# An attention and MLP kernel: the rows' normalization factors gathered in one tile, turned by TensorE and stored in one transfer

## The chip, the cores and the metric

The kernel runs on one core of a Trainium2 chip. The metric is the device time of one execution in microseconds (us). The page of the profile and the trace come from one execution; the times of the runs stand beside it. Engines are named as in the profile: PE is TensorE (matrix products; PEld its weight loads), DVE is VectorE, ACT is ScalarE, POOL is GpSimd, and SP is SyncE, which here only issues transfers. A name with a q behind it (SPq, POOLq) is that engine's issuing of transfers.

## What is computed

For 2048 rows of 640 features, a normalized copy of the input goes into two branches, and both are added to the input. One branch is attention with 32 heads of 20 features, the other a second normalization and a two-layer network of width 1536 with GELU.

```python
def reference(A_x, A_wqkv, A_wo, B_x, B_w1, B_b1, B_w2, B_b2):
    x = A_x                                   # 1 x 2048 x 640
    xn = _layernorm(x, axis=-1)
    return x + _A_ref(xn, A_wqkv, A_wo) + _B_ref(xn, B_w1, B_b1, B_w2, B_b2)

    # _A_ref: softmax(q k^T / sqrt(20)) v per head, times wo
    # _B_ref: y = _layernorm(x); gelu(y w1 + b1) w2 + b2
```

The second normalization works on rows that are normalized already, so it is one factor per row. That factor is applied late, to the product with w1, and it is what this change is about.

## The kernel before

**Numbers in halves.** Most products are made of pairs of 16-bit floats (a high and a low half), three products each.

**The projection stage** takes about the first 224 us. The rows are handled in four chunks of 512 (c = 0 to 3). For each chunk a loop over tt = 0 to 4 makes five pairs of 128 output features of q and k (`qk`, 30 matrix products of 128x512, L337, into PSUM tiles `qkp`); behind it, a loop over j = 0 to 3 makes v for 128 rows at a time (`vproj`, 30 products of 128x320, L410, into tiles `vp`). Both use the PSUM pool `psS`, which has three buffers, so a product must wait until the tile three before it has been read. `qk_out` reads a finished `qkp`: ACT writes the high half (L352), DVE the low half (L353) into a tile `qkhl` of two buffers, and SP stores both halves to `qkscr` in HBM (L358). A new `qkhl` can be written only when the store of the one two before it has landed.

**The next chunk's rows** are made ready during a chunk. `norm_a`, `norm_b` and `norm_c` compute mean and variance of 4 x 128 rows, the first factor (tile `r`), the normalized rows, and the second factor (tile `r2`, 128 x 4: row 128 j + p of the chunk is at partition p, column j). `turn` splits normalized rows in halves (tile `row`, three buffers, L318 and L319) and turns them with a DMA transpose into `xnt` (L320), of which a copy goes to HBM (`xscr`, L323). Chunk 0 runs its own norm steps ahead of the loops and inside the first one; chunk 1's run in chunk 0, chunk 2's in chunk 1, chunk 3's in chunk 2.

**The weights** of the MLP are split into halves on ACT and DVE in small pieces between these steps (`some`, `weights`, `split`, L139 to L141); the output weights `wos` are fetched by POOL (L506) for their scale.

**The factors' way.** At the end of `norm_c`, POOL stores the chunk's 512 factors to the HBM tensor `rscr` (L286). In HBM they are to stand in the order of the rows, while in the tile neighbouring rows stand in neighbouring partitions, so the store consists of 512 elements of four bytes. `load_chunk` fetches 256 of them at a time (L1015), spread over all 128 partitions, as `r2f`. The first two loads are issued by SP at 220 us, ahead of the attention stage; L989 and L966 use them.

**The attention stage** (from about 224 us) makes scores (L748), exponentials on ACT (L750), low halves on DVE (L762) and the products with v (L779), 64 blocks of heads and rows; the MLP's two products (L1031 and L1061) are strewn between them by a plan that is fixed when the program is built. The output product (L1146) ends the kernel.

**Order.** The instructions of each engine run in the order in which the program is written (manual schedule); engines wait for each other through semaphores. SP's and POOL's transfers are issued in order too: a transfer whose inputs aren't ready holds those behind it.

Of the kernel before, what the change touches and what calls it, by code (L numbers as in the profile page):

```python
# [9 lines left out]
F32 = mybir.dt.float32  # L10
# [8 lines left out]
P = 128  # L19
S, D, H, DH, F = 2048, 640, 32, 20, 1536  # L20
KD = D // P
KF = F // P
NKB = S // P
# [16 lines left out]
MC = 256  # L40
# [4 lines left out]
def mha_mlp_kernel(tc, x, wqkv, wo, w1, b1, w2, b2, out):  # L45
    nc = tc.nc
# [3 lines left out]
    with (  # L50
# [8 lines left out]
    ):  # L59
        qkscr = dram.tile([2, 2 * D, S], F16, name="qkscr")  # L60
        xscr = dram.tile([P, KD, 2, S], F16, name="xscr")
        rscr = dram.tile([S], F32, name="rscr")
        oscr = dram.tile([2, D, S], F16, name="oscr")
        opart = dram.tile([2, D, S], F32, name="opart")
        lpart = dram.tile([2, 2, H, S // 2], F32, name="lpart")
# [13 lines left out]
        ident = keep.tile([P, P], F32, name="ident")  # L79
# [95 lines left out]
        with tc.tile_pool(name="pa", bufs=2) as pa, tc.tile_pool(name="pa1", bufs=1) as pa1, tc.manual_schedule():  # L175
# [59 lines left out]
                    nc.tensor.matmul(ps[:, :P], ones, ones, start=True, stop=True)  # L235

            rs = {}

            def newton(dst, v, pref, by=1.0):
                t = pa.tile([P, 4], F32, tag=pref + "t", name=pref + "t")  # L240
                nc.vector.tensor_mul(t, dst, dst)
                nc.vector.scalar_tensor_tensor(t, v, -0.5 * by, t, ALU.mult, ALU.mult)
                nc.vector.scalar_tensor_tensor(dst, t, 1.5 * by, dst, ALU.add, ALU.mult)

            def norm_a(c, between=None):

                xt = xts[c]
                st = pa.tile([P, 4, 2, 6], F32, tag="st", name="st")
                mv = pa.tile([P, 4, 2], F32, tag="mv", name="mv")
                ve = pa.tile([P, 4], F32, tag="ve", name="ve")  # L250
                r = pa.tile([P, 4], F32, tag="r", name="r")
                r2 = pa.tile([P, 4], F32, tag="r2", name="r2")
                for j in range(4):
                    for i in range(2):
                        nc.vector.bn_stats(st[:, j, i, :], xt[j][:, i * 320 : (i + 1) * 320])  # L255
                    nc.vector.bn_aggr(mv[:, j, :], st[:, j])
                nc.vector.tensor_scalar(ve, mv[:, :, 1], EPS, None, ALU.add)
                if c == 0:
                    between()
                    nc.scalar.activation(r, mv[:, :, 1], AF.Sqrt, bias=eps)  # L260
                    nc.vector.reciprocal(r, r)
                else:
                    nc.gpsimd.tensor_tensor(r, ve, nhalf, ALU.pow)
                rs[c] = mv, ve, r, r2
# [18 lines left out]
            def norm_c(c):  # L283
                mv, ve, r, r2 = rs.pop(c)
                newton(r2, ve, "b")
                nc.gpsimd.dma_start(rscr[c * 512 : (c + 1) * 512].rearrange("(j p) -> p j", p=P), r2)  # L286

            xnts = {}

# [56 lines left out]
            def qk_out(c, tt, ps):  # L346
                hl = stp.tile([P, 2, 2, 512], F16, tag="ks", name="qkhl")

                parts = ((0, 2),) if tt != 2 else ((0, 1), (1, 2))
                for i0, i1 in parts:  # L350
                    a = qks[:, (2 * tt + i0) // KD : (2 * tt + i0) // KD + 1]
                    nc.scalar.activation(hl[:, 0, i0:i1], ps[:, i0:i1], AF.Copy, scale=a)  # L352
                    nc.vector.scalar_tensor_tensor(hl[:, 1, i0:i1], ps[:, i0:i1], a, hl[:, 0, i0:i1],  # L353
                                                   ALU.mult, ALU.subtract)
                if c + tt > 0:
                    qk_sq(c, tt, hl)
                for s in range(2):
                    nc.sync.dma_start(  # L358
                        qkscr[s, 2 * tt * P : (2 * tt + 2) * P, c * 512 : (c + 1) * 512]
                        .rearrange("(i p) t -> p i t", p=P), hl[:, s])  # L360
                return hl

            def qk_sq(c, tt, hl):
                if tt % 2:
                    sq = stp.tile([P, S // 2], F16, tag="qs", name="sq").bitcast(BF16).rearrange("p (i t) -> p i t", i=2)
                else:
                    sq = pa.tile([P, 2, 512], BF16, tag="sq", name="sq", bufs=2)
                if c == 0:
                    nc.scalar.activation(sq, hl[:, 0], AF.Square)
                else:  # L370
                    nc.vector.tensor_mul(sq, hl[:, 0], hl[:, 0])
                pend.extend((c, 2 * tt + i, sq[:, i]) for i in range(2))
# [56 lines left out]
            def sums(tag, ws):  # L429
                accs[tag] = squares(ws, junk)  # L430
# [154 lines left out]
            for c in range(4):  # L585
                nxt = c + 1 if c < 3 else None
                for tt in range(5):
                    if c == 0 and tt == 1:
                        norm_b2(0)
                        norm_c(0)  # L590

                        nc.scalar.activation(junk[:, :1], ones[:, :1], AF.Exp)
                        ps = qk(0, 1, lambda: scale_of("k"))
                        hl = qk_out(0, 0, first)
                        split_qkv("q", c0=4 * P)
                        split_qkv("k")
                    else:
                        ps = qk(c, tt)
                    if tt == 3:
                        lengths(4)  # L600

                    if c == 0:
                        if tt == 0:
                            split_qkv("q", c0=2 * P, c1=4 * P)
                            sums("k", [stage["k"][:, 0:3], stage["k"][:, 3:]])
                            first = ps
                            continue
                        elif tt == 1:
                            qk_sq(0, 0, hl)
                        elif tt == 2:  # L610
                            sums("v", [stage["v"][:, 0:3], stage["v"][:, 3:]])
                            norm_a(1)
                        elif tt == 3:
                            scale_of("v")
                            split_qkv("v")
                    else:

                        step = tt - (c == 1)
                        if nxt and 0 <= step < 3:
                            (norm_a, norm_b, norm_c)[step](nxt)  # L620
                            some(1)
                        else:
                            some(2)
                    qk_out(c, tt, ps)

                    ask((0, 1, 2, 2, 1)[tt] if c == 0 else 0)
                    if nxt and c > 0 and tt >= 2:
                        for j in ((0,), (1, 2), (3,))[tt - 2]:
                            turn(nxt, j)
                    if c == 3 and tt == 2:  # L630
                        early = [load_features(mc) for mc in range(2)]
                if c == 1:
                    load_x(3)
                if c == 3:
                    stack = load_stack(0, 0)
                    for _ in range(6):
                        next(stack)
                for j in range(4):
                    ps = vproj(c, j)
                    if j == (0 if c == 3 else 1):  # L640
                        lengths(10)
                    if c + j > 0:

                        vproj_out(c, j, ps)
                    if c == 0:
                        if j < 2:
                            (norm_b, norm_c)[j](1)

                        pts = []
                        for k in ((), (0,), (2, 4), ())[j]:  # L650
                            transp(1, k, pts)
                        for t in pts:
                            transp_out(*t)
                    if j == 0 and c == 3:
                        shifts()
                        for _ in stack:
                            pass
                    some(1 if c == 3 else 2 if j < 3 or c == 0 else 0)
                    if c + j == 0:
                        vproj_out(c, j, ps)  # L660
                    if c == 0:
                        ask(2 if j == 0 else 1)
                if c == 0:
                    load_x(2)
# [3 lines left out]
        with ExitStack() as scope:  # L668
# [342 lines left out]
            def load_chunk(mc):  # L1011
                t0 = mc * MC
                xnt = early.pop(0) if early else load_features(mc)
                r2f = m1.tile([P, MC], F32, tag="r2f", name="r2f", bufs=2)
                nc.sync.dma_start(r2f, rscr[None, t0 : t0 + MC].to_broadcast([P, MC]))  # L1015
                xs[mc] = xnt, r2f
                unscaled.append(r2f)
                if mc > 1:
                    patient.append(scale_ahead(r2f))
# [323 lines left out]
```

The loop that calls them, cut:

```python
            for c in range(4):                                  # L585
                nxt = c + 1 if c < 3 else None
                for tt in range(5):
...
                        step = tt - (c == 1)
                        if nxt and 0 <= step < 3:
                            (norm_a, norm_b, norm_c)[step](nxt)
                            some(1)
                        else:
                            some(2)
                    qk_out(c, tt, ps)
```

## Time and profile before

| | us |
|---|---|
| runs (three) | 1332.33, 1337.95, 1342.94 |
| median | 1337.95 |
| profiled execution, span | 1337.9 |
| projection stage, 0 to 235 us: PE, DVE, ACT busy | 228.0, 146.2, 122.3 |
| attention, 235 to 1275 us: PE, DVE, ACT busy | 1039.6, 887.2, 1005.1 |
| end, 1275 to 1337.9 us: PE, DVE, ACT busy | 58.2, 21.6, 0.6 |
| mean granted clock of PE | 0.997 |

The profiled execution has no other time of its own than its span, which is within 0.05 us of the median of the runs. Busy time counts instructions at work, not waiting ones. "x12" behind a name is a count of instructions; "[3.67 <-DVE qkhl L353]" says that the engine was idle for 3.67 us before the instruction, and that an instruction of line 353 on DVE ended this.

### The profile page before, as it was taken

To read this page: it belongs to the slowest core of one execution; us is meant where nothing else is said; L and a number is where in the kernel's file an instruction comes from. 1 tells how busy PE (TensorE), PEld (TensorE's weight loads), DVE (VectorE), ACT (ScalarE), POOL (GpSimd) and SP (SyncE) were. 2 spreads that over 40 slices of the span, in tenths; PEclk is the share of its full clock that TensorE was granted. 3 is DMA by queue.
4 is the path that set the end of the run, shared out by engine and by line. 5 is a ranking of instruction groups with operands and counts; after the bars stand their busy time and mean duration, and the time that the engine had idled before them with its cause. 6 is when DMAs were issued, how large, how long until landed. Compare 5 with 4: busy or idle time off the path is not lost.

```text
span 1337.9 us, 29042 instructions
## 1 busy us (share of the span) xinstructions
PE 1325.8 (99%) x11635; PEld 586.7 (44%) x11635; DVE 1055.1 (79%) x1431; ACT 1128.0 (84%) x1306; POOL 37.5 (3%) x86
## 2 busy tenths in 40 slices
PE   9999899999999999999999999999999999999998
PEld 6645456444434343434343443344443434333366
DVE  7656754998788989878897879888879888997742
ACT  7844334999999999999999999999999999999900
POOL 3010000000000000000000000000000000000000
PEclk9999899999999999999999999999999999999999
DMA  9778723021203232212322132223032323334375
GB/s 279 254 196 176 136 79 104 15 59 39 66 28 103 61 83 81 63 48 59 111 63 81 33 93 66 75 69 94 19 80 71 93 66 87 118 95 118 105 218 188
DMA packets 100326, 129.54 MB, mean 97 GB/s; under 512 B 24292, under 2 KB 66664, under 8 KB 100188
## 3 DMA queue, kind: packets, MB, share of 16 engines
q1 hardware_dynamic: 96652, 120.25, 31.6%
q0 software_dynamic: 2912, 6.90, 2.8%
q8 instruction: 92, 1.51, 0.5%
q10 hardware_dynamic: 624, 0.51, 0.1%
q14 instruction: 46, 0.38, 0.1%
HBM read 82.14 MB, written 42.51 MB: 93 GB/s over the span
## 4 chain that ended last, share of the span: by engine, by line
PE 87%; DVE 6%; DMA 4%; ACT 1%; issue 1%; SPq 0%; ACTq 0%; DVEq 0%
PE o L779 30%; PE s L748 20%; PE py L1061 13%; PE pu L1031 11%; PE z L1146 5%; PE qkp L337 5%; PE vp L410 3%; DVE low L762 2%; DMA xt<-in_A_x_dram 1%; DMA xnt<-row 1%; DMA qkscr<-qkhl 1%; DVE st L255 1%; DVE qkhl L353 1%; ACT p L750 1%; DMA wos<-in_A_wo_dram 0%
## 5 line engine op out<-in xcount | busy, mean ns | idle before, releaser
L750 ACT ACTIVATE p<-s 128x1024 f32<-128x1024 f32 x1024 | 973.9, 1050 | 33.1 <-PE s L748 27.1
L762 DVE TENSOR_TENSOR low<-p 128x1024 f16<-128x1024 f32 x512 | 614.3, 1218 | 144.8 <-ACT p L750 144.0
L779 PE MATMUL o<-p,vfull 128*32 128x512 bf16 (+1 forms) x4096 | 429.0, 493 | 0.0
L748 PE MATMUL s<-qs,ks 61*128 61x512 f16 x2048 | 311.4, 381 | 0.2 <-ACT p L750 0.2
L748 PEld LDWEIGHTS <-ks 61*128 61x128 f16 x2048 | 61.2, 94 | 278.4 <-issue 276.1
L1061 PE MATMUL py<-w2t,hT 128*128 128x320 f16 x1152 | 178.5, 300 | 0.0
L1031 PE MATMUL pu<-xm,w1t 128*128 128x256 f16 x1440 | 178.2, 273 | 0.1
L1031 PEld LDWEIGHTS <-w1t 128*128 128x128 f16 x1440 | 131.0, 98 | 64.0 <-issue 50.2
L1061 PEld LDWEIGHTS <-hT 128*128 128x128 f16 x1152 | 102.3, 98 | 88.1 <-issue 53.9
L337 PE MATMUL qkp<-xnt,wv 128*128 128x512 f16 x600 | 131.1, 379 | 1.3 <-issue 1.3
L779 PEld LDWEIGHTS <-vfull 128*32 128x32 f16 x3072 | 59.9, 95 | 138.4 <-issue 106.9
L779 PE MATMUL o<-low,vfull 128*32 128x512 f16 x1024 | 101.3, 377 | 0.1
L337 PEld LDWEIGHTS <-wv 128*128 128x128 f16 x600 | 58.2, 98 | 71.0 <-issue 1.6
L779 PEld LDWEIGHTS o<-p,vfull 128*32 128x32 f32 x2048 | 61.7, 108 | 53.2
L410 PE MATMUL vp<-wv,xnt 128*128 128x320 f16 x480 | 69.5, 306 | 3.7 <-DVE qkhl L353 3.7
L1146 PE MATMUL z<-w1t,ot 128*128 128x320 f16 x480 | 67.4, 299 | 0.0
L352 ACT ACTIVATE qkhl<-qkp,qks 128x1024 f16<-128x1024 f32 (+1 forms) x24 | 23.1, 964 | 46.3 <-PE qkp L337 26.6
L410 PEld LDWEIGHTS <-xnt 128*128 128x128 f16 x480 | 47.9, 100 | 23.8 <-issue 3.7
L1146 PEld LDWEIGHTS <-ot 128*128 128x128 f16 x480 | 46.0, 98 | 22.9 <-issue 5.5
L353 DVE SCALAR_TENSOR_TENSOR qkhl<-qkp,qks,qkhl 128x1024 f16<-128x1024 f32 (+1 forms) x24 | 26.5, 1104 | 32.9 <-ACT qkhl L352 32.9
L1103 DVE SCALAR_TENSOR_TENSOR acc<-z,sc,acc 128x320 f32<-128x320 f32 x32 | 17.5, 549 | 37.3 <-PE z L1146 37.2
L800 ACT ACTIVATE ev<-o 128x512 f32<-128x512 f32 x64 | 39.5, 618 | 2.2 <-PE o L779 2.1
(195 smaller groups left out, 670.4 us busy)
## 6 DMA issues: line engine op xcount, KB each, us to landing
qkscr<-qkhl SPq DMA_DIRECT2D x40, 256.0 KB
opart<-ev SPq DMA_DIRECT2D x124, 80.0 KB
ks<-qkscr SPq DMA_DIRECT2D x120, 80.0 KB
qs<-qkscr SPq DMA_DIRECT2D x192, 40.0 KB
oa<-opart SPq DMA_DIRECT2D x32, 240.0 KB
xt<-in_A_x_dram SPq DMA_DIRECT2D x16, 320.0 KB
xscr<-xnt SPq DMA_DIRECT2D x4, 1280.0 KB
xm<-xscr SPq DMA_DIRECT2D x8, 640.0 KB
```

Of the source, the lines that this page charges most:

```text
L337: nc.tensor.matmul(ps[:, i, :], wv[:, k, q, a, mm * P : (mm + 1) * P], xnts[c][:, k, b, :], start=(k + n == 0), stop=(k == KD - 1 and n == 2))
L352: nc.scalar.activation(hl[:, 0, i0:i1], ps[:, i0:i1], AF.Copy, scale=a)
L353: nc.vector.scalar_tensor_tensor(hl[:, 1, i0:i1], ps[:, i0:i1], a, hl[:, 0, i0:i1], ALU.mult, ALU.subtract)
L410: nc.tensor.matmul(ps[:, hf, :320], xnts[c][:, k, a, j * P : (j + 1) * P], wv[:, k, 2, b, hf * 320 : (hf + 1) * 320], start=(n == 0), stop ...
L748: nc.tensor.matmul(ps[:, a, :], ks[64 * a : 64 * a + 61, kb * P : (kb + 1) * P], qs[64 * a : 64 * a + 61, cc * 512 : (cc + 1) * 512], star ...
L750: nc.scalar.activation(pt, ps, AF.Exp, scale=QS)
L762: nc.vector.tensor_sub(low, pt, upper(pt))
L779: nc.tensor.matmul(pv.o[32 * q : 32 * q + 32, :], src[:, v0 - PAD * (1 - q % 2) :][:, :32], t, start=q not in pv.begun, stop=last, skip_gr ...
L800: nc.scalar.activation(evs[g, hf][:, cc], pv.o, AF.Copy)
L1031: nc.tensor.matmul(ps[:, i], w1v[:, k, (f + i) // 4, a, fo_ : fo_ + P], xnt[:, k, b, :], start=(n == 0), stop=(n == 3 * KD - 1))
L1061: nc.tensor.matmul(ps[:, :320], hTs[mc][:, f, a, j * P : (j + 1) * P], w2v[:, f, b, hf * 320 : (hf + 1) * 320], start=(n == 0), stop=(n == ...
L1146: nc.tensor.matmul(ps[:, :320], ot[:, k, a, j * P : (j + 1) * P], wov[:, k, b, h * 320 : (h + 1) * 320], start=(n == 0), stop=(n == 3 * KD ...
```

## The change

`rscr` becomes a tensor of 16 x 128 (the same bytes in the same order). One tile `rall` of 128 x 16 takes the place of the four tiles `r2`: chunk c computes its factors in columns 4c to 4c+3. `norm_c` no longer stores. A new function, `factors_out`, is called once, in the last chunk behind the second group of q and k (c = 3, tt = 1): PE turns `rall` into a PSUM tile `pr` of 16 x 128, DVE copies it to `rrow`, and POOL stores that in 16 rows of 512 bytes. The eight loads of `r2f` read the same places as before.

```diff
-        rscr = dram.tile([S], F32, name="rscr")
+        rscr = dram.tile([NKB, P], F32, name="rscr")
...
             rs = {}
+            rall = pa1.tile([P, NKB], F32, name="rall")
...
-                r2 = pa.tile([P, 4], F32, tag="r2", name="r2")
+                r2 = rall[:, 4 * c : 4 * c + 4]
...
             def norm_c(c):
                 mv, ve, r, r2 = rs.pop(c)
                 newton(r2, ve, "b")
-                nc.gpsimd.dma_start(rscr[c * 512 : (c + 1) * 512].rearrange("(j p) -> p j", p=P), r2)
+
+            def factors_out():
+
+                pr = psM.tile([P, 512], F32, tag="m", name="pr")[:NKB, :P]
+                nc.tensor.transpose(pr, rall, ident)
+                rrow = sm.tile([NKB, P], F32, tag="rrow", name="rrow", bufs=1)
+                nc.vector.tensor_copy(rrow, pr)
+                nc.gpsimd.dma_start(rscr, rrow)
...
                     qk_out(c, tt, ps)
+                    if c == 3 and tt == 1:
+                        factors_out()
...
-                nc.sync.dma_start(r2f, rscr[None, t0 : t0 + MC].to_broadcast([P, MC]))
+                nc.sync.dma_start(r2f, rscr.rearrange("j p -> (j p)")[None, t0 : t0 + MC].to_broadcast([P, MC]))
```

Lines behind L285 carry numbers that are 8 higher in the changed kernel (L353 is L361 there), lines behind L624 numbers that are 10 higher.

## The prediction

> **What bounds the kernel now.** I read the head of the page first, then the waits of the first 235 us, the chain of waits there, stages of 4 us, and last the tile that the change touches.
>
> ```profile
> span 1337.9 us, 29042 instructions
> PE 1325.8 (99%) x11635; PEld 586.7 (44%) x11635; DVE 1055.1 (79%) x1431; ACT 1128.0 (84%) x1306; POOL 37.5 (3%) x86
> PEclk9999899999999999999999999999999999999999
> ```
>
> TensorE (PE) works 1325.8 of 1337.9 us, so only 12.1 us of the span is PE idle time. Whatever a change gains must come out of those 12.1 us or out of stretches with a lower clock, and the clock row dips once, in the fifth slice (134 to 167 us). That lies in the projection stage, where all four stores of the rows' factors lie too.
>
> ```profile
> ACT qkhl L352 <- DMA qkscr<-qkhl: 6.3, 1, 6.3
> PE vp L410 <- DVE qkhl L353: 3.7, 1, 3.7
> ACT row L318 <- DMA xnt<-row: 6.5, 1, 6.5
> ```
>
> These are waits of the first 235 us (total, times, longest). PE's largest wait in the stage, 3.7 us, is on VectorE (DVE), not on a transfer. The chain of waits leads further back; its columns are start, duration, what:
>
> ```profile
> 138.86 12.66 DMA qkscr<-qkhl
> ...
> 151.63 1.12 ACT qkhl L352
> ...
> 152.77 1.28 DVE qkhl L353
> ...
> 158.17 1.29 DVE qkhl L353
> ...
> 159.50 6.88 PE vp L410 x30
> ...
> 207.91 4.08 PE vp L410 x30
> ```
>
> A store of q and k halves (L358), issued at 138.86, needed 12.66 us. ScalarE (ACT) could not refill that buffer before 151.63; DVE then ran late through its queue, its next qkhl ended at 159.46, and the PSUM buffer that the second vp block needs came free only then. The block itself took 6.88 us, while 30 equal matmuls at 207.91 took 4.08.
>
> Why did a 256 KB store need 12.66 us? The stages show PE, weight load, DVE, ACT and POOL busy, then clock, DMA share, GB/s:
>
> ```profile
> 24.00:28.00 4.00, 4.00 (x22) 1.98 (x20) 2.56 (x11) 3.97 (x11) 0.81 (x1) 1.00 1.06 373
> 28.00:32.00 4.00, 4.00 (x21) 1.73 (x19) 4.00 (x9) 4.00 (x7) 0.00 (x0) 1.00 1.01 98
> ...
> 60.00:64.00 4.00, 4.00 (x34) 3.27 (x33) 0.27 (x2) 3.39 (x6) 0.00 (x0) 1.00 1.01 402
> 64.00:68.00 4.00, 4.00 (x30) 2.72 (x29) 2.14 (x6) 3.61 (x7) 0.00 (x0) 1.00 0.57 104
> ...
> 100.00:104.00 4.00, 4.00 (x31) 2.96 (x30) 3.13 (x15) 1.11 (x1) 0.00 (x0) 1.00 1.12 27
> ...
> 148.00:152.00 4.00, 4.00 (x21) 1.96 (x20) 0.00 (x0) 0.37 (x1) 0.00 (x0) 1.00 1.14 43
> ...
> 156.00:160.00 4.00, 0.50 (x3) 0.27 (x3) 3.93 (x8) 2.76 (x5) 0.00 (x0) 0.76 0.92 183
> 160.00:164.00 4.00, 4.00 (x17) 2.27 (x16) 3.79 (x13) 0.00 (x0) 0.00 (x0) 0.50 0.75 194
> 164.00:168.00 4.00, 4.00 (x47) 2.62 (x46) 2.12 (x6) 1.58 (x3) 0.00 (x0) 0.88 0.64 215
> ```
>
> ```profile
> L286 POOL DMA_DIRECT2D rscr<-r x4: 767/791/812, 24.6 to 140.2; - x4
> ...
> DMA to landing us min/median/max: 11.4/11.6/12.5
> ...
> 58.70 0.79 POOL L286 DMA_DIRECT2D rscr<-r  x1 [3.54 <-DVE r L243]
> ...
> 94.74 0.79 POOL L286 DMA_DIRECT2D rscr<-r  x1 [3.21 <-DVE lo L117]
> ```
>
> Four times the throughput falls to between 27 and 104 GB/s. Two of these times the share of busy DMA time is still above 1, so packets are under way and do not finish. The four stores of factors, 2 KB each as 512 elements of four bytes, were issued at 24.6, 58.70, 94.74 and 140.2, and each took 11.4 to 12.5 us: every drop lies inside one of them. Two of the four cost PE nothing that I can see: it is busy 4.00 of 4.00 at 28 to 32 and 64 to 68 us.
>
> **The change, part by part.** First the removed stores. The last one issues 1.3 us after the qkscr store that then needs 12.66 us. Gone with it is the 3.67 us of PE idle time, in the first row here (time, duration, work, idle time before it):
>
> ```profile
> 159.50 6.88 PE L410 MATMUL vp<-wv,xnt 128*128 128x320 f16 x30 [3.67 <-DVE qkhl L353]
> ...
> 118.66 3.61 PE L337 MATMUL qkp<-xnt,wv 128*128 128x512 f16 x16 [1.26 <-issue]
> ```
>
> and with it the clock loss behind the idle time: the block's 6.88 against 4.08 is 2.80 us. The stage table checks this: half clock for 4 us costs 2.0, 0.88 for 4 us another 0.5, and 0.50 us of work at a lower clock in the stage before about 0.25, together 2.7.
>
> The Trainium skill, "TensorE: Matmul & The Clock Gate", Part 1 (the HAM clock gate), says that PE falls to half its clock after an idle window of about 3.4 us. The trace agrees: 3.67 us idle was followed by a clock of 0.50, and 1.26 us idle by no dip.
>
> The third store (94.74) was in flight while ACT waited 6.5 us at 108 us for a DMA transpose to release its row buffer. The last transpose of the block of rows came late through that, and PE waited 1.26 us at 118.66 for it. I count that as gone too: ACT's 6.5 us of lateness is over five times the 1.26.
>
> What is late next where the stall was?
>
> ```profile
> 144.99 6.65 PE L337 MATMUL qkp<-xnt,wv 128*128 128x512 f16 x30
> ...
> 155.55 0.28 PE L114 MATMUL mxp<-acco,ones 128*128 128x5 f32 x2
> ```
>
> Without the wait ACT takes up qkhl about 6.3 us earlier, at 145.3 instead of 151.63, and DVE follows. The next qkhl then waits only for its own matmuls, which end at 151.6; with 1.12 us on ACT and 1.28 on DVE it ends at about 154.1, before PE wants that buffer, at 155.8 behind the mxp pair. So the cover is 1.7 us, and what eats more than that comes back as PE idle time one for one.
>
> Now what is added. PE gets one turn of 128x16 floats, in the last chunk, between its second and third group of qkp. VectorE, from the two listings, before and after, around that place (last chunk, second group; qkhl are halves of q and k, w1t weights being split):
>
> ```order
> L353 SCALAR_TENSOR_TENSOR qkhl<-qkp,qks,qkhl 128x1024
> L371 TENSOR_TENSOR sq<-qkhl 128x1024
> L140 CAST w1t<-wtmp 128x512
> L141 TENSOR_TENSOR w1t<-wtmp,w1t 128x512
> L353 SCALAR_TENSOR_TENSOR qkhl<-qkp,qks,qkhl 128x512 x2
> ```
>
> ```order
> L361 SCALAR_TENSOR_TENSOR qkhl<-qkp,qks,qkhl 128x1024
> L379 TENSOR_TENSOR sq<-qkhl 128x1024
> L293 COPY rrow<-pr 16x128
> L140 CAST w1t<-wtmp 128x512
> L141 TENSOR_TENSOR w1t<-wtmp,w1t 128x512
> ```
>
> The copy stands behind the qkhl that itself waits for the matmuls ahead of the turn, so it waits for nothing new; behind it are queued the weight splits and the next qkhl. GpSimd (POOL), before and after:
>
> ```order
> L281 TENSOR_TENSOR r_935<-ve,nhalf 128x4
> L286 DMA rscr<-r_935 128x4x1
> L506 DMA wos<-in_A_wo_dram 128x640 x4
> L263 TENSOR_TENSOR r<-ve,nhalf 128x4
> L281 TENSOR_TENSOR r_1404<-ve,nhalf 128x4
> L506 DMA wos<-in_A_wo_dram 128x640
> L286 DMA rscr<-r_1404 128x4x1
> ```
>
> ```order
> L282 TENSOR_TENSOR rall<-ve,nhalf 128x4
> L514 DMA wos<-in_A_wo_dram 128x640 x4
> L264 TENSOR_TENSOR r<-ve,nhalf 128x4
> L282 TENSOR_TENSOR rall<-ve,nhalf 128x4
> L514 DMA wos<-in_A_wo_dram 128x640
> L294 DMA rscr<-rrow 16x128
> ```
>
> Four stores leave POOL's queue and one stands last; the first wos load no longer waits behind a store for DVE's factors. The rows that price the new work:
>
> ```profile
> 56.74 1.02 PE pt L299 x8
> ...
> 174.93 26.06 PE L337 MATMUL qkp<-xnt,wv 128*128 128x512 f16 x120
> ...
> 189.23 1.28 DVE L353 SCALAR_TENSOR_TENSOR qkhl<-qkp,qks,qkhl 128x1024 f16<-128x1024 f32 x1 [2.46 <-ACT qkhl L352]
> 190.43 0.68 DVE L371 TENSOR_TENSOR sq<-qkhl 128x1024 bf16<-128x1024 f16 x1
> ...
> 195.28 0.75 DVE L353 SCALAR_TENSOR_TENSOR qkhl<-qkp,qks,qkhl 128x512 f16<-128x512 f32 x1 [2.04 <-ACT qkhl L352]
> ...
> 212.21 0.57 DVE L386 TENSOR_REDUCE lmx<-norms 128x1 f32<-128x128 f32 x2 [1.18 <-PE norms L382]
> ...
> bscr<-brow POOLq DMA_DIRECT2D x1, 4.0 KB, 5.4
> ```
>
> The turn: eight turns of 128x128 floats take 1.02 us, so one takes 0.13. It is on the path, and I count 0.13 in full; the ends are 0 and 0.28 (twice that and more, if PE's pipeline breaks). The copy: half of the pair of reads of 128x128 floats from PSUM, 0.57/2 = 0.29 us, an upper bound for 16 rows; the 2.04 us that DVE idles before its next qkhl hide it. Without that cover it would be 0.29. The new store goes between the nearest small POOL store of long runs (5.4 us to landing) and the old ones (12.5); it is hidden either way, see the third rival.
>
> The sum for the profiled execution: 1337.9 - 3.67 - 2.80 - 1.26 + 0.13 = **1330.3 us**. Its span and the median of the runs, 1337.95, differ by 0.05, so the sum carries over. The rest of the kernel follows one for one: from 235 us on PE is the engine that never waits, until the last 63 us.
>
> **The rivals.** *The stores are not what holds the others.* The drops at 100 and 148 us also hold DMA transposes. If these are the cause, ACT waits as before and only queue places move: -0.5 to -1.3 from the wait at 118.66, so 1336.7 to 1337.9. If the qkscr store is sped up by only half of the 6.3, the idle of 3.67 shrinks to about 0.5 and the clock loss goes: 1331. Against the rival: at 28 to 36 us no transpose is issued, and the drop is the same; and with transposes but no store, at 156 to 164 us, the engines move 183 and 194 GB/s. Chance 0.14.
>
> The Trainium skill, "DMA: Bandwidth & Descriptors", section "Anatomy of one DMA — SWDGE (gpsimd) path", fits such a transfer as about 2.0 us plus bytes over 436 GB/s, which would make each old store 2.0 us and speak for this rival. The measured 11.4 us speaks against it.
>
> *The single late store holds the loads (slower).* All eight loads of factors (r2f, L1015) now depend on one store.
>
> ```profile
> L1015 SPq DMA_DIRECT2D r2f<-rscr x8: 353/358/1070, 220.2 to 905.4; - x8
> ...
> 231.26 0.35 DVE L989 TENSOR_SCALAR r2f<-r2f,sc 128x256 f32<-128x256 f32 x1
> ```
>
> The turn follows half of the 120 matmuls from 174.93, so about 188.0; the copy ends at 191.1 + 0.3; with 0.8 us of POOL and the worst landing of 12.5 the store is down at 204.7, and SyncE reads it at 220.2. The margin is 15.5 us, and 26.5 to the first use at 231.26. Only a landing past 231 makes PE wait, and it must be past about 252 to outweigh the gain of 7.6 and cost 1% besides: 1352 us. Nothing in the rows has such a latency. Chance 0.03.
>
> *More is won than the profile shows.* The runs reach 1342.94, so other executions may hold bigger stalls; and all remaining idle time, start and end, bounds the gain. The two stages behind 235 us:
>
> ```profile
> 235.00:1275.00 1040.00, 1039.59 (x9746) 415.64 (x9745) 887.22 (x1057) 1005.11 (x1125) 15.00 (x18) 1.00 0.26 73
> 1275.00:1337.90 62.90, 58.23 (x445) 42.19 (x441) 21.61 (x44) 0.60 (x1) 0.00 (x0) 0.98 0.68 208
> ```
>
> The last holds 4.67 us of idle, the one before 0.41, the first 25 us hold 12.1 - 3.67 - 1.26 - 4.67 - 0.41 = 2.1. Without them too: 1323.5. The first store comes at 24.6 and the last at 140.2, so neither should move. Chance 0.06.
>
> **How the numbers follow.** The forecast, stall and dip gone, has 0.77, the rivals 0.14, 0.03 and 0.06. The runs before lie 5 us around their median, so a median of a few runs carries about 3 us either way: the forecast covers 1326 to 1335, and with the first rival and the edge of the last the range is 1325 to 1338. One per cent, about what a measurement of this kernel tells from no change, is 13.4 us: under 1324.6 or over 1351.3. The forecast's gain is 0.57%, inside it. Faster: the last rival's 0.06 and 0.02 of the forecast's edge, 0.08; slower: 0.03; within 1%: 0.89.
>
> **What would show it.** Right: no drop under 110 GB/s with a share near 1 in the first 160 us; qkscr stores that land in a few us; no ACT wait on qkscr; PE idle under 0.5 us between 25 and 235 us; clock 1.00 in every slice; PE busy still about 1323 (2.8 less). Wrong: a clock dip near 150 us with the stores gone, PE idle behind the turn or in front of the first scores, or a SyncE wait at L1015.

## The result and the profile after

| | before | after |
|---|---|---|
| runs, median (us) | 1337.85 (22 runs, 1332.33 to 1342.94) | 1332.34 (22 runs) |
| profiled execution: span / own time (us) | 1337.9 / not listed | 1330.2 / 1332.15 |
| PE busy in the span (us) | 1325.8 | 1323.6 |
| mean clock of PE | 0.997 | 0.999 |

The ratio of the changed kernel to the one before is 0.9969, 95% interval 0.9956 to 0.9981: a small gain that is clear of noise, and inside the one per cent that was forecast. (One run of the changed kernel took 2230.65 us at a clock of 0.629; it is left out of the ratio.) The medians lie 5.5 us apart, the ratio amounts to 4.1 us. The spread changed more than the middle: of the 21 other runs after, all lie between 1332.05 and 1335.35, while nine of the 22 before are over 1339.

The head of the page after; they answer to the lines shown of before:

```profile
span 1330.2 us, 29036 instructions
PE 1323.6 (100%) x11636; PEld 586.9 (44%) x11636; DVE 1055.4 (79%) x1432; ACT 1128.5 (85%) x1306; POOL 34.9 (3%) x83
PEclk9999999999999999999999999999999999999999
```

The dip in the clock row is gone. PE busy is 2.2 us shorter though PE has one instruction more: the half-speed stretch is what went.

Stages of the projection after (PE, weight loads, DVE, ACT, POOL busy; clock, DMA share, GB/s), and last the stretch in which the four stores lay, as one stage:

```profile
28.00:32.00 4.00, 4.00 (x20) 1.79 (x19) 4.00 (x9) 4.00 (x6) 0.00 (x0) 1.00 0.28 99
32.00:36.00 4.00, 4.00 (x21) 1.79 (x19) 3.54 (x7) 3.97 (x4) 0.00 (x0) 1.00 0.24 86
...
64.00:68.00 4.00, 4.00 (x30) 2.70 (x29) 2.13 (x6) 3.61 (x7) 0.00 (x0) 1.00 0.36 125
...
100.00:104.00 4.00, 4.00 (x32) 2.94 (x31) 3.26 (x15) 1.74 (x2) 0.00 (x0) 1.00 0.82 190
...
148.00:152.00 4.00, 4.00 (x26) 2.37 (x25) 2.94 (x6) 1.74 (x2) 0.00 (x0) 1.00 0.88 164
...
25.00:235.00 210.00, 210.00 (x1393) 115.00 (x1393) 137.97 (x293) 113.48 (x157) 10.30 (x14) 1.00 0.51 157
```

PE is busy for all 210 us between 25 and 235. At 100 and 148 us the throughput is 190 and 164 GB/s where it was 27 and 43. At 28 to 36 us it is as low as before (99 and 86 GB/s against 98 and 91) with no store in flight, and at 64 us nearly so (125 against 104); what fell there is the share, at 28 us from 1.01 to 0.28 and at 64 us from 0.57 to 0.36. So the low throughput of these two stages was mostly lack of work, and the store merely filled the share. A high share with few bytes says that slow packets are under way; that they hold something else shows only in a transfer that lands late.

The turn, the copy and the store, from the timeline after (start, duration) and the view of the tile `rscr`:

```profile
179.86 0.27 PE L291 MATMUL pr<-ident,rall 128*16 128x128 f32 x1
...
183.01 0.27 DVE L293 COPY rrow<-pr 16x128 f32<-16x128 f32 x1
...
183.58 0.52 POOL L294 DMA_DIRECT2D rscr<-rrow  x1 [47.76 <-DVE rrow L293]
```

```profile
L1025 SPq DMA_DIRECT2D r2f<-rscr x8: 352/358/1311, 212.0 to 897.5; - x8
...
DMA to landing us min/median/max: 1.6/1.6/1.6
```

The store lands 1.6 us after its issue, 27 us before SP reads the factors at 212.0. And where the stall was, from the chain of waits:

```profile
150.09 4.08 PE vp L418 x30
154.16 0.12 PE mxp L114 x2
154.28 4.09 PE vp L418 x30
...
180.03 0.11 PE pr L291
```

The second vp block follows the first at once and takes 4.09 us, not 6.88. In the chain the turn is worth 0.11 us.

The other signs that the prediction named are there too: in the first 160 us no stage of 4 us with a share over 0.7 moves less than 164 GB/s, ACT waits for no qkscr store, and PE has no idle time behind the turn or ahead of the first scores. How fast the qkscr stores of this run land is in none of the views shown.

### The profile page after: what moved, and what is told of

Same layout as the page of the kernel before. It is cut to its first block, busy times and chain, and to the rows that moved or that the text cites. A ratio compares the mean times of both kernels' runs of the same rounds, so it can differ in the third digit from the quotient of the medians.

```text
span 1330.2 us, 29036 instructions
## 1 busy us (share of the span) xinstructions
PE 1323.6 (100%) x11636; PEld 586.9 (44%) x11636; DVE 1055.4 (79%) x1432; ACT 1128.5 (85%) x1306; POOL 34.9 (3%) x83
## 4 chain that ended last, share of the span: by engine, by line
PE 95%; DVE 3%; ACT 1%; issue 0%; DVEq 0%; POOL 0%; ACTq 0%; POOLq 0%
PE o L789 30%; PE s L758 20%; PE pu L1041 12%; PE py L1071 12%; PE qkp L345 10%; PE z L1156 5%; PE vp L418 5%; DVE low L772 2%; PE warm L235 1%; ACT p L760 1%; PE norms L390 0%; DVE w1t L730 0%; PE rb L941 0%; DVE wtmp L725 0%; PE pt L307 0%
## 5 line engine op out<-in xcount | busy, mean ns | idle before, releaser
L418 PE MATMUL vp<-wv,xnt 128*128 128x320 f16 x480 | 66.8, 299 | 0.0
L361 DVE SCALAR_TENSOR_TENSOR qkhl<-qkp,qks,qkhl 128x1024 f16<-128x1024 f32 (+1 forms) x24 | 26.5, 1105 | 28.3 <-ACT qkhl L360 28.2
```

The costliest lines, as they stand in the source:

```text
L418: nc.tensor.matmul(ps[:, hf, :320], xnts[c][:, k, a, j * P : (j + 1) * P], wv[:, k, 2, b, hf * 320 : (hf + 1) * 320], start=(n == 0), stop ...
```

## The experiments

Twelve runs, the kernel before once more and eleven variants, each beside runs of the kernel before in the same session. The theory: the stores of four-byte elements hold the DMA engines, other transfers with them, and through ACT and DVE finally PE. The rivals: the DMA transposes hold them; the change of POOL's queue (the first wos load) is what helped; or GpSimd's software queue is at fault, not the elements. Where a variant ran only once, no interval is given. The changed kernel itself did not run in these sessions; its 1332.34 us is from the section above.

**The kernel before, once more** (no edit).

> The kernel before, unchanged, once more, because its runs spread over 10 us (1332 to 1343) where the changed kernel's spread over 2 to 3. Theory (the four-byte stores hold the others): the wait of ACT on a qkscr store after the fourth store, the PE idle time behind it and the clock dip are there again, and their size differs between executions; span = about 1326.5 plus the idle time in the 25 to 235 us stretch plus the clock loss plus the idle at both ends. Rival (something else spreads the runs): the stall is 3.7 us again whatever the span is, and a different span comes from another stage.

It took 1334.47 us (span 1332.4). Waits of its first 235 us, the stage of the stall, and a piece of its chain:

```profile
ACT row L318 <- DMA xnt<-row: 7.0, 1, 7.0
DVE row L319 <- ACT row L318: 3.9, 1, 3.9
ACT qkhl L352 <- DMA qkscr<-qkhl: 3.4, 1, 3.4
PE vp L410 <- DVE qkhl L353: 1.5, 1, 1.5
```

```profile
130.00:170.00 40.00, 38.48 (x261) 21.87 (x259) 34.33 (x71) 18.55 (x28) 3.71 (x4) 1.00 0.69 140
```

```profile
144.69 8.77 DMA qkscr<-qkhl
...
153.56 1.12 ACT qkhl L352
...
156.05 4.24 PE vp L410 x30
```

The stall is there again, but it is another and a smaller one. ACT's wait on qkscr is 3.4 us instead of 6.3 and falls on the next `qkhl`: the held store is one issued 3.2 us behind the fourth store of factors (at 141.54 here), where in the first trace it was issued 1.3 us ahead of it. PE's idle time before the vp block is 1.5 us instead of 3.7, the clock stays at 1.00, and the 1.26 us at 118.66 are not there at all. Against the first trace the span is 5.5 us shorter: 3.4 from PE's idle time in this stage, 1.9 from its busy time (1323.9 us against 1325.8), the rest elsewhere. So the size of this stall differs between executions, as the theory had it. Two traces don't show that this is the whole spread of the runs, but the clocks of the runs speak for it: of the 57 runs of the kernel before in the three sessions of these experiments, the six over 1339 us have a mean clock of 0.996 or 0.997, and all under 1335 us have 0.998 to 1.000.

**The fourth store issued twice** (doubling the suspected cost).

```diff
                 nc.gpsimd.dma_start(rscr[c * 512 : (c + 1) * 512].rearrange("(j p) -> p j", p=P), r2)
+                if c == 3:
+                    nc.gpsimd.dma_start(rdup.rearrange("(j p) -> p j", p=P), r2)
```

> The kernel before, with the fourth store issued twice, the second time to an unused place in HBM. Theory (the engines of the transfers are held for as long as such a store lasts): the qkscr store beside it needs 17 to 22 us, ACT waits 10 to 14 us, PE idle 8 to 12 us, and a longer clock dip; own time 6 to 10 us over the kernel before. Rival (the transposes or other transfers hold the qkscr store): 12 to 14 us as before, and the time of the kernel before within 1 us.

1345.41 us against 1336.25 (ratio 1.0085, 1.0056 to 1.0114). The waits, and the landing of the two stores (last column):

```profile
ACT qkhl L355 <- DMA qkscr<-qkhl: 13.8, 2, 13.0
PE vp L413 <- DVE qkhl L356: 10.8, 1, 10.8
```

```profile
rscr<-r POOLq DMA_DIRECT2D x4, 2.0 KB, 12.7
...
rdup<-r POOLq DMA_DIRECT2D x1, 2.0 KB, 19.5
```

Twice the store, and the qkscr store that ACT waits for needs 18.4 us, PE waits 10.8, and the run takes 9.2 us more by the medians (11.4 by the ratio). The expectation was 17 to 22, 8 to 12 and 6 to 10 us. The transposes are the same eight, so the added time is the added store's: the stores hold the others.

**One old store or two old stores in the changed kernel.** Three variants keep the old form at the old place for the last chunk, for the first three, or for the third and the fourth, and turn and store the remaining columns.

```diff
                 newton(r2, ve, "b")
+                if c == 3:      # the other two: c < 3, and c > 1
+                    nc.gpsimd.dma_start(rscr[4 * c : 4 * c + 4].rearrange("j p -> p j"), r2)
```

> The changed kernel, but the last chunk's 512 factors are stored at the old place in 512 elements of four bytes; the other three chunks' factors are turned and stored as in the changed kernel. Theory (this store beside the qkscr store makes the stall): a qkscr store over 9 us again, ACT waits 4 to 7 us on it, PE idle 2 to 4 us near 150 us, perhaps a clock dip; own time 1334.5 to 1339. Rival (the gain came from POOL's queue, whose first wos load no longer stands behind a store, or from the transposes being earlier): no wait on qkscr, as the changed kernel, 1332 to 1333.

> The changed kernel, but the first three chunks' factors are stored at the old places in elements of four bytes; only the last chunk's are turned and stored in four rows. Theory: no stall near 150 us and no clock dip; ACT's wait of about 6 us on the DMA transpose near 102 to 108 us is back, PE idle 0.5 to 1.5 us near 118; own time 1332.5 to 1334. Rival (all four stores count alike, a fourth of the gain each): 1336 to 1337.

> The changed kernel, but the third and the fourth chunk's factors are stored at the old places in elements of four bytes; those of the first two are turned and stored. Theory (the stall needs both: the third store makes ACT, DVE and the last row loads late by a few us, and only then does the fourth store's wait reach PE; the first two cost nothing): ACT waits about 6 us on the DMA transpose near 102 and 3 to 6 us on qkscr near 148; in some executions PE idle 1 to 4 us and a clock dip; own times spread like those of the kernel before, from 1332 to 1340. Rival (the stall needs all four, or comes by chance to any variant): the median within 0.5 us of the changed kernel's and no run over 1335.

They took 1332.14, 1332.49 and 1332.18 us in the median of ten runs each; of the 30 runs one, with the last store old, took 1340.71, all others at most 1333.99. The ratios to the kernel before are 0.9983 (0.9964 to 1.0002), 0.9975 (0.9961 to 0.9989) and 0.9973 (0.9958 to 0.9988). Last store old, a wait and the stage:

```profile
ACT qkhl L362 <- DMA qkscr<-qkhl: 3.5, 1, 3.5
...
130.00:170.00 40.00, 40.00 (x268) 22.48 (x267) 31.96 (x65) 19.14 (x28) 2.51 (x3) 1.00 0.68 134
```

ACT waits on qkscr, but PE is busy for 40 of 40 us, where I had expected it to wait 2 to 4 us and the run to take 1334.5 or more; the time is the rival's. ACT's wait ends at 150.32, and the matmuls that it needs had ended only at 150.15, so it comes out of the wait just 0.2 us late. The run of 1340.71 us has no trace, so what it lost stays open; its clock is 0.997, as in the slowest runs of before. With the first three old, PE's idle time in the stage behind them is 0.65 us, within what I had expected:

```profile
ACT row L328 <- DMA xnt<-row: 7.6, 1, 7.6
...
110.00:130.00 20.00, 19.35 (x112) 10.60 (x110) 14.20 (x29) 12.27 (x21) 1.62 (x3) 1.00 1.01 266
```

With the third and the fourth old, ACT waits 2.0 us for a transpose and 2.4 us for a qkscr store, and PE does not wait at all:

```profile
ACT qkhl L362 <- DMA qkscr<-qkhl: 2.4, 1, 2.4
ACT row L328 <- DMA xnt<-row: 2.0, 1, 2.0
```

The wait of 2.4 us ends at 130.59, before the fourth store is issued at 135.99, so it isn't that store's; behind the fourth store ACT waits for no transfer here. This contradicts my expectation of the last variant, that the third and fourth store together bring the spread back; the signs of its rival came out, that the stall needs all four or comes by chance. What is missing is lateness from ahead of the third store. When VectorE can start on the third chunk's rows depends on it; the first BN_STATS of that chunk (for mean and variance) in the kernel before, and in this variant, where the first two stores are gone:

```profile
81.17 0.89 DVE L255 BATCH_NORM_STATS2 st<-xt 128x6 f32<-128x320 f32 x2 [4.27 <-DMA xt<-in_A_x_dram]
```

```profile
78.45 0.89 DVE L256 BATCH_NORM_STATS2 st<-xt 128x6 f32<-128x320 f32 x2 [1.34 <-DMA xt<-in_A_x_dram]
```

2.7 us earlier. It is so in every trace: in the four with GpSimd's second store in the old form this instruction starts at 81.06 to 82.20, in the nine without it at 76.58 to 78.93, and with that store on SyncE's queue (the next variant) at 80.02. It waits for a load of `xt` that needs 12.8 us in the kernel before, and between 68 and 72 us, where that load begins and the second store ends, the throughput is 146 GB/s before and 277 after.

The first store adds nothing up to there: GpSimd takes up the second chunk's factors at 54.16 before and at 54.03 after. With the second store gone, the third (92.10 instead of 94.74) and the fourth go out earlier, and ACT's wait on the transpose is 2.0 us where it is 7.6 with the first three old. Over four traces the fourth store was issued at 135.99, 137.50, 140.19 and 141.54 us, and ACT then waited for qkscr 0, 3.5, 6.3 and 3.4 us. So what the fourth store costs hangs on when it meets the qkscr stores, and the stores before it shift that moment. That the second one does this by itself is argued: no variant leaves out the second store alone. The rival of the second variant, that all four stores count alike (1336 to 1337 us), fell.

**SyncE's queue in place of GpSimd's** (`nc.gpsimd` becomes `nc.sync` in the store of the kernel before).

> The kernel before, but the four stores of four-byte elements are issued by SyncE on its hardware queue and no longer by GpSimd. Theory (the elements' number and size hold the transfers): the stalls stay, ACT waits 4 to 7 us on qkscr near 145 us, PE idle 2 to 4 us; own time 1335 to 1342. Rival (GpSimd's software queue, with its descriptors, is what holds them): landing under 4 us, no such wait, 1332 to 1333.

1332.04 us against 1334.19 (ratio 0.9984, 0.9970 to 0.9998), no wait of ACT on qkscr or on a transpose. That is what the rival expects of the software queue. But the stores block transfers in this run too, as its stages show:

```profile
100.00:104.00 4.00, 4.00 (x31) 2.96 (x30) 3.15 (x15) 1.74 (x2) 0.00 (x0) 1.00 1.37 15
140.00:144.00 4.00, 4.00 (x35) 1.72 (x33) 3.93 (x7) 3.29 (x6) 0.00 (x0) 1.00 1.07 72
```

At 100 us it is 15 GB/s at a share of 1.37, worse than the 27 at 1.12 of the kernel before; the changed kernel moves 190 there, and 152 at 140 us. So SyncE's queue doesn't free the others, only it costs ACT no wait and PE no time. Why not is argued: on SyncE's queue the store can't overtake the transfers issued ahead of it, as in this piece of the timeline:

```profile
136.15 0.37 SPq L358 DMA_DIRECT2D qkscr<-qkhl  x1
...
137.21 0.37 SPq L286 DMA_DIRECT2D rscr<-r  x1
```

Queue and order are mixed in this edit. So two more variants of the changed kernel put one unused store of 512 elements at the same moment, ahead of the second qkscr store of that group:

```diff
                 for s in range(2):
+                    if (c, tt, s) == (2, 1, 1):
+                        d = sm.tile([P, 4], F32, tag="d", name="d")
+                        nc.vector.tensor_copy(d, hl[:, 1, 1, 0:4])
+                        nc.sync.dma_start(fa.rearrange("j p -> p j"), d)   # or nc.gpsimd
                     nc.sync.dma_start(
```

> The changed kernel with one more store of 512 elements of four bytes to an unused place, issued by SyncE directly ahead of the second qkscr store of group two in the third chunk (its values are not used). Theory A (such elements hold whatever is behind them, on either kind of queue; the variant with SyncE's stores did not wait because the sensitive transfers stood ahead of them in the same queue): ACT waits 2 to 7 us on qkscr near 145 us. Theory B (only GpSimd's software queue holds the others): no such wait, as in the changed kernel.

> The same store at the same moment, issued by GpSimd. Both theories: ACT waits 2 to 7 us on qkscr near 145 us. No wait would say that the moment, not the queue, decides.

On SyncE's queue:

```profile
136.60 0.37 SPq L370 DMA_DIRECT2D fa<-d  x1
...
137.02 7.69 SPq L371 DMA_DIRECT2D qkscr<-qkhl  x3
...
ACT qkhl L361 <- DMA qkscr<-qkhl: 5.6, 1, 5.6
...
PE vp L423 <- DVE qkhl L362: 1.5, 1, 1.5
```

ACT waits 5.6 us and PE 1.5, and the qkscr store behind the unused one needed 10.9 us: a store on the hardware queue holds others too, at least those behind it. Issued by GpSimd at the same 136.60 us, there is no wait on qkscr at all, which neither theory had expected. Transfers are blocked there as well (58 GB/s at a share of 1.12 between 144 and 148 us, where the changed kernel moves 194 at 0.72), but ACT needs none of them at that time. So the kind of queue is not the cause, and a store costs time only at a moment when somebody needs the transfers beside it.

**One late store of 2048 elements** (no turn and no copy):

```diff
-                pr = psM.tile([P, 512], F32, tag="m", name="pr")[:NKB, :P]
-                nc.tensor.transpose(pr, rall, ident)
-                rrow = sm.tile([NKB, P], F32, tag="rrow", name="rrow", bufs=1)
-                nc.vector.tensor_copy(rrow, pr)
-                nc.gpsimd.dma_start(rscr, rrow)
+                nc.gpsimd.dma_start(rscr.rearrange("j p -> p j"), rall)
```

> The changed kernel without the turn and the copy: at the same place the gathered tile is stored in one transfer of 2048 elements of four bytes. Theory (time goes by the number of elements): 512 took 11.4 to 12.5 us, so 2048 land after 25 to 48 us, at 208 to 230 us; qkscr stores of the last chunk come late, and the factors' loads at 212 wait; own time 1335 to 1350. Rival (being gathered and late is what helps, the elements are free where few transfers run): as the changed kernel, 1332 to 1333.

1332.65 us (ratio 0.9993, 0.9982 to 1.0004), where I had expected 1335 or more. The place was not the one that I had assumed: without the copy nothing holds GpSimd, and it issued the store at 138 us, beside the same qkscr stores as before.

```profile
138.38 1.19 POOL L290 DMA_DIRECT2D rscr<-rall  x1 [2.00 <-DVE rall L244]
...
ACT qkhl L356 <- DMA qkscr<-qkhl: 4.5, 1, 4.5
```

Four times the elements, and ACT waits 4.5 us where it waited 3.5 for 512, far from four times as long. PE is busy for 40 of the 40 us from 130 on. So this variant, with no row of 512 bytes, takes the time of the changed kernel to 0.3 us, which says that for the time it is enough to be without the first three stores. Its interval includes 1, as that of the last store alone does, so these two are not shown to be faster than the kernel before in their own sessions.

**The landing of such stores by themselves.** Two kernels add unused stores where few transfers run.

```diff
+                    if c == 3 and tt in (0, 2, 3):
+                        d = sm.tile([P, 4], F32, tag="d", name="d")
+                        nc.vector.tensor_copy(d, hl[:, 1, 1, 0:4])
+                        nc.gpsimd.dma_start({0: fa.rearrange("j p -> p j"), 2: fb[:, :, 0], 3: fc}[tt], d)
```

> The changed kernel with three more stores by GpSimd in the last chunk, where few transfers run, each of a 128x4 tile of floats (its contents are not used): (a) 512 elements of four bytes in the order of the rows, so that neighbouring partitions write neighbouring words; (b) 512 elements of four bytes, each 512 bytes from the next; (c) 128 runs of 16 bytes. Theory (the number of elements counts): (a) and (b) land alike, after 6 to 12 us, (c) after 2 to 4 us. Rival (neighbouring words written from different engines collide): (a) 6 to 12 us, (b) and (c) 2 to 4 us.

> The changed kernel with three more stores of four-byte elements by GpSimd at quiet places (their contents are not used): 128 elements that are neighbours in HBM, 2048 elements that are neighbours, and 2048 elements 512 bytes apart. The store of 512 neighbours landed after 9.2 us, of 512 elements 512 bytes apart after 4.5 us, of 128 runs of 16 bytes after 2.0 us. Theory (a cost for each element, and more where neighbouring words come from different partitions): 128 neighbours 3 to 4 us, 2048 neighbours 25 to 35 us, 2048 apart 11 to 16 us. Rival (neighbouring words collide only within a row of 512 bytes, and rows go in parallel): 128 neighbours about 9 us, 2048 neighbours 9 to 14 us.

The issues of transfers, with KB and us to landing, of the first and of the second kernel: `fa` 512 neighbours, `fb` 512 elements 512 bytes apart, `fc` 128 runs of 16 bytes; `ff` 128 neighbours, `fd` 2048 neighbours, `fh` 2048 elements 512 bytes apart.

```profile
fa<-d POOLq DMA_DIRECT2D x1, 2.0 KB, 9.2
...
fb<-d POOLq DMA_DIRECT2D x1, 2.0 KB, 4.5
fc<-d POOLq DMA_DIRECT2D x1, 2.0 KB, 2.0
```

```profile
ff<-d POOLq DMA_DIRECT2D x1, 0.5 KB, 9.3
...
fd<-d POOLq DMA_DIRECT2D x1, 8.0 KB, 14.6
fh<-d POOLq DMA_DIRECT2D x1, 8.0 KB, 5.2
```

128 neighbours need as long as 512 (9.3 and 9.2 us), while 2048 elements that lie 512 bytes apart need 5.2. The theory of a cost per element falls here, and the rival of the second kernel holds nearly: neighbouring words of a row of 512 bytes, written from different partitions, are what takes the time, and several rows go side by side (4 as fast as one, 16 in 14.6 us, a little over its 14). In the first kernel the 4.5 us of `fb` lie in neither expectation. Why neighbours are slow isn't settled by this: runs of 16 bytes are neighbours too, and land after 2.0 us. They are a quarter as many writes to a row, and a quarter of 9.2 us is 2.3; that the number of writes to one row counts is an estimate from these two, not shown.

**Each chunk for itself**, turned and stored in four rows of 512 bytes, soon after its factors are there:

```diff
-                    if c == 3 and tt == 1:
-                        factors_out()
+                    if (c, tt) in PLACES:      # ((0, 3), (1, 0), (1, 4), (2, 3))
+                        factors_out(PLACES.index((c, tt)))
```

> The changed kernel, but each chunk's factors are turned, copied and stored for themselves (four turns, four copies, four stores of 4 rows of 512 bytes, each about one group of products after the factors are there). Theory (rows of 512 bytes are what helps, not that it is one transfer or late): no ACT wait on qkscr or on the transposes over 2 us, PE idle under 0.5 us between 25 and 235 us, own time as the changed kernel plus 0 to 0.6 us, 1332 to 1333.5. Rival (fewer transfers or the late place are what helps): 1334 or more, with part of the waits back.

1332.61 us (ratio 0.9988, 0.9976 to 1.0000), no wait of ACT on qkscr or a transpose, PE busy throughout that stretch. The four stores, with the median of their landing:

```profile
rscr<-rrow POOLq DMA_DIRECT2D x4, 2.0 KB, 3.1
```

That it is one transfer adds nothing that can be measured. Rows of 512 bytes take ACT's waits away, which the one store of 2048 elements left at 4.5 us. These four stores stand 8 to 25 us behind the old ones, so form and place aren't wholly separated.

No variant is clearly better than the changed kernel: with PE busy for all of 25 to 235 us there is nothing left in this stage for a store to give. The other rival, GpSimd's queue with the first wos load, has nothing for it: ACT waits 6.2 us in all for wos before and after. Over all sessions 42 of 79 runs of the kernel before took more than 1335 us, but one of 21 of the changed kernel and one of the 60 of the six variants that ran ten times.

## Why the prediction was right, and where not

**The bound** held: nearly the whole gain came from PE idle time and the clock dip, in the stage that was named, and from 235 us on nothing moved (PE is busy 1039.5 of 1040 us against 1039.6).

**The cause** held in one part and failed in another. The stores hold the qkscr store: doubling the fourth one gave the 10.8 us of idle, with the same transposes. But "every drop lies inside one of them" took the low throughput at 28 to 36 and at 64 us for a blockage; most of it is there without the store. With it goes the prediction's argument against its first rival, that the drop at 28 to 36 us is the same without transposes. A share above 1 it counts in two of the four stages; its own rows have three (1.01, 1.12 and 1.14).

**The removed terms** (3.67, 2.80 and 1.26 us) are all gone from the profiled execution: idle 0.00 in 25 to 235 us, no dip, span 1330.2 where the sum gave 1330.3. That it fits to 0.1 us is luck in part: PE's busy time fell by 2.2 us and not by 2.67, and its idle time in the first 25 us by 0.8, which nothing in the change explains. What failed is how the terms were assigned to single stores. I gave 1.26 to the third and 6.47 to the fourth and said that the first two cost PE nothing. With the fourth alone the ten runs' median is that of the changed kernel to 0.2 us, with the third and fourth too; VectorE is 2.7 us late where the second store stands, and of the traces with old stores on GpSimd's queue only those with all four show idle time ahead of the vp block. The sum came out all the same because the change removes all four. The 1.26 us at 118.66 are not in the second trace of before, so they are no fixed cost of the third store either. The clock term goes by all or nothing: 3.67 us of idle time brought the dip, 1.5 in the second trace of before did not. The Trainium skill, "TensorE: Matmul & The Clock Gate", Part 1, has half the clock after an idle window of about 3.4 us, and these two agree with it.

**What is late next**: this step was right in size. After, ACT's qkhl waits 3.33 us for nothing but its matmuls, DVE ends it at 152.55, and the next vp block starts at 154.28 with no gap: a cover of 1.7 us, as worked out. And beyond it the lateness does come back one for one. Against the end of its matmuls ACT takes up that qkhl 1.2 us late with the one store of 2048 elements, and PE waits for nothing; 3.2 us late in the second trace of before, and PE waits 1.5; 12.5 us late with the store doubled, and PE waits 10.8.

**The added terms** were small as forecast: the turn 0.11 us in the chain (0.13 forecast), the copy 0.27 (at most 0.29) and hidden. The store's landing was bounded from 5.4 to 12.5 us and was 1.6: the nearest row, of the same queue but from the busy first microseconds (8.1 us), was no good neighbour.

**The sum's base** is the step that was off in size. The text said that the profiled execution's span is its own time and near the median, so the sum carries over. The runs after list both: 1332.15 us of time for a span of 1330.2, so about 2 us lie around the span; a later run of the kernel before with the same span of 1337.9 took 1339.85. Before's profiled execution therefore took about 1339.9 us, among the slower ones of that kernel's 22 runs, and that its span met the median to 0.05 us was chance. The sum from that base is 1332.2, which is the median after to 0.1; but against the median of before it is a gain of 5.5 us, not 7.6, and by the ratio 4.1. The profile had shown a stall bigger than usual.

**The rivals**: the transposes as the cause fell (doubled store; no blockage after). The fit of the Trainium skill, "DMA: Bandwidth & Descriptors", section "Anatomy of one DMA — SWDGE (gpsimd) path", of 2.0 us and little for the bytes is near the store of 16 rows (1.6) and the runs of 16 bytes (2.0), and misses the neighbouring words (9.2). The late store never held the loads: it was down 27 us ahead, more than the 15.5 that were worked out. More than the profile shows was not won.

## What to carry to other kernels

Look for stretches where the DMA share is high and the bytes are few; then see which small transfer is in flight, and whether the busiest engine loses time by a transfer beside it: at 28 us of this kernel, and with the stores on SyncE's queue, PE lost none. A store that writes neighbouring words from different partitions is worth a turn on TensorE when transfers that someone waits for run beside it, and gains nothing where there is slack. Before a stall is priced from one trace, a second trace of the same kernel tells whether its size is typical, and stalls from several small delays can't be assigned to one of them by taking its last wait.

## What the runs showed of the hardware

The landing of a small store is set by the pattern of its addresses more than by its elements: 9.3 us for 128 neighbouring words, 9.2 for 512 and 14.6 for 2048, but 4.5 and 5.2 for 512 and 2048 words that lie 512 bytes apart, 2.0 for 128 runs of 16 bytes, and 1.6 for 16 rows of 512 bytes (each in one trace). While a store of neighbouring words is in flight, other transfers slow down, on either kind of queue: 27 GB/s at a share of 1.12 beside GpSimd's and 15 at 1.37 beside SyncE's, both at 100 us; a qkscr store needed 12.7 us beside GpSimd's, 18.4 beside two of them, and 10.9 behind one on SyncE's own queue.
